# VectorE's exponential as two bf16 tiles that TensorE sums, in a pre-LN attention and GeGLU block

## The chip, the cores and the metric

The kernel runs on one core of one Trainium2 chip. The core has a matrix engine (TensorE, PE in the profile; PEld is its weight load), a vector engine (VectorE, DVE), an engine for functions such as the exponential (ScalarE, ACT), a general engine (GpSimd, POOL) and SyncE (SP), which here only issues DMAs. The metric is device time in microseconds of one execution; the time before is the median of three runs.

## The reference

One transformer block over a sequence of S = 2048 rows of D = 640, with 32 heads of 20, and a gated feed-forward part of width 1728, all in bf16:

```python
x = A_x
h = x + _A_ref(_layernorm(x, axis=-1), A_wqkv, A_wo)
h2 = h + _B_ref(_layernorm(h, axis=-1), B_w_gate, B_w_up, B_w_down)
# _A_ref: qkv = x @ wqkv; scores = q k^T * 20 ** -0.5; p = softmax(scores)
#         o = p v; o @ wo
# _B_ref: g = x @ w_gate; u = x @ w_up; (gelu_tanh(g) * u) @ w_down
```

The exponentials are the bulk of the elementwise work: 32 x 2048 x 2048 of them, which are 2048 tiles of 128 keys by 512 queries.

## The kernel before

The kernel lists its operations with their dependencies, planned durations and priorities, and a planner inside it (`Sched.schedule`) walks through planned time and fixes the order of instructions on each engine and the PSUM bank of each result. On the chip every engine then runs its own list in order and waits on semaphores. Almost every instruction is issued from one place, so most groups of the profile carry the line of that helper (L429); the matmuls of QK are at L1072, the evacuations on VectorE of its share of the scores at L996, gate and up at L1275, down at L1393.

Attention goes by **slots** (33 of them). A slot is a range of queries and one or more groups of four heads: 512 queries and one group, 256 and two, or 128 and four; each holds 16 **quads**, and a quad is four tiles, one for each head of a group. The scores of a tile are one bank of PSUM. TensorE computes QK with the four heads in four row strips of its array (contraction 32) and PV in four column strips (21 output rows: 20 of the head and one of ones, which gives the softmax's sum). The bound that takes the place of the row maximum enters through one extra row of Q, with the constant `OFF`.

Most tiles go to ScalarE in **units** of three and two tiles alternately (banks 0 to 2 and 3 to 4; two and two in slots 28 and 29): one Exp of 1536 or 1024 columns each (`unit`). Some quads go to VectorE instead. `D_QUADS` says how many in each slot, `D_LEAD` how many tiles ahead of their slot they start, and `D_LAG` how many units after a quad's last QK its PV is put into the list. Such a tile uses bank 7 or 5, which it shares with the background matmuls. `d_exp` evacuates it as int16: the scaled score is an exponent and a mantissa's fraction in fixed point. Two tiles, or from slot 16 on four, are then corrected together in five or six more instructions: mask the fraction, a linear step, a square, a product, an addition to the integer, and a last scaling that makes the bits of a bf16 number. In the slots named in `DA_SLOTS` the addition is done by a DMA that GpSimd issues and that accumulates in SBUF (`accum_op=ALU.add`). PV then takes the one bf16 tile (`pv_op`).

The feed-forward part of a chunk of rows (six **chunks** of 256 and four of 128) is background work that fills TensorE's and VectorE's lists between the attention's slots (`post`, `down`). Its GELU has three forms. In plain form the gate matmuls are copied to SBUF and ScalarE runs GELU in long instructions, with a load of another function table ahead of and behind it; chunks in `MERGE` hold their gates until the next chunk's are there, so that both share the loads. Chunks in `TANH` use tanh, which shares a table with Exp, and some more instructions on VectorE. The last chunk (the tail) runs after the last exponential.

Where the planner finds TensorE too idle for its clock to stay up, it adds filler matmuls of zeros to the PV accumulation (`pad`, in the profile `ps<-kt_all,zer`) or to a free bank (`warm`).

Of the kernel before, what the change touches and what calls it, by code (L numbers as in the profile page):

```python
# [7 lines left out]
ALU = mybir.AluOpType  # L8
# [362 lines left out]
OFF = 63.0 * 0.6931471805599453 / SCALE  # L371

OCT = 512.0
EXP_MUL = SCALE * 1.4426950408889634 * OCT
CA, CB, CC = -0.277383, 1.25604202, 1.0 - 11.0 / 128
PV_QUADS = 2
D_LAG = 12
MERGE = (0, 2)
TANH = (4, 6, 7, 8)
# [7 lines left out]
DA_ISSUE, DA_LAT = 0.95, 7  # L387
DA_SLOTS = (1, 10, 11, 12, 14, 15, 16, 18, 19, 20, 22, 23, 27, 28, 31)
PR, PR2 = 12, 6
D_QUADS = (0, 2, 2, 2, 2, 2, 2, 2, 2, 2, 2, 2, 3, 2, 3, 2, 3, 2, 3, 2, 3, 2, 3, 2, 2, 2, 3, 2, 3, 2, 2, 2, 0)  # L390
D_FIRST, D_PART = 2, 0.55
D_LEAD = ((0, 0, 0, 0, 0, 0, 0, 0), (0, 10, 20, 36, 36, 36, 36, 40, 36, 36, 32, 36, 36, 36, 36, 36, 40, 36, 32, 36, 40, 36, 36, 32, 36))
D_WIDE = 16
D_G = (7, 8)
# [13 lines left out]
def bass_sequential_preLN__mha_block__glu_gated_geglu__prompt_kernel(  # L408
# [12 lines left out]
    with ExitStack() as es:  # L421
# [93 lines left out]
        dv = [ka[:, 1024 * i:1024 * i + 1024].bitcast(I16) for i in range(2)]  # L515
        dvw = [ka.bitcast(I16)]
        pts2 = carve(PR2 * 512)


        carve = carver(qt_all[:, 0, :, :].rearrange("p g s -> p (g s)"), NG * 512)  # L520
        dv += [carve(1024).bitcast(I16) for _ in range(2)]
        df1 = carve(1024)
        dw1 = [carve(1024), dwx[:, 1024:2048]]
        carve = carver(qt_all[:, 0, :, :].rearrange("p g s -> p (g s)"), NG * 512)
        dvw += [carve(2048).bitcast(I16) for _ in range(2)]
        dv += [dvx[:, 1024 * i:1024 * i + 1024].bitcast(I16) for i in range(2)]
        dvw.append(dvx[:].bitcast(I16))
        zb = dvx[:, 0:1024].rearrange("p (i s) -> p i s", i=2)
        dv0 = [ha_f[:, 1024 * i:1024 * i + 1024].bitcast(I16) for i in range(5)]
        dv0.append(hnT.rearrange("p a s -> p (a s)")[:, 1024:2048].bitcast(I16))  # L530
        df0 = ha_f[:, 5120:6144]
        dw0 = [ha_f[:, 6144:7168], hnT.rearrange("p a s -> p (a s)")[:, 0:1024]]
        carve = carver(qt_all[:, 1, :, :].rearrange("p g s -> p (g s)"), NG * 512)
        df2 = carve(2048)
        dw2 = [carve(2048), dwx[:]]
        carve = carver(qt_all[:, 2, :, :].rearrange("p g s -> p (g s)"), NG * 512)
        dvw += [carve(2048).bitcast(I16) for _ in range(2)]
# [404 lines left out]
        d_cur, d_now = [None], [None]  # L942
        d_alt = [0]
        d_late = []
# [11 lines left out]
        def q_done(k):  # L956
            return sum((tuple(last_qk[c]) for c, (q0, _) in enumerate(QR) if q0 // 512 == k), ())

        def d_kind(tile, u):
            if tile[0] in (7, 8) and units[u][0][0] in D_G:  # L960
                return "g"
            return "e" if tile[0] < e_end else "f" if tile[0] < 8 else "l" if tile[0] < D_WIDE else "w"

        def d_free(tile):
            kind = d_now[0]
            return sum((tuple(sc.rd.get((x, t), ())) for x in ("aq", "sel") for t in range(NA)), ()) if kind == "g" else \
                tuple(sc.rd.get(("aq", 2), ())) + tuple(sc.rd.get(("aq", 3), ())) if kind == "l" else \
                tuple(t_last.get(4, ())) if kind == "w" and d_cur[0][1] > 3 else ()

        def d_pick(tile, u):  # L970
            if len(d_raw) == 0:
                d_now[0] = kind = d_kind(tile, u)
                busy = set(x[1][1] for x in d_done)
                busy |= set(("w", k) for k, ks in enumerate(((0, 1), (2, 3), (), (4, 5))) if any(("l", x) in busy for x in ks))
                n_ = {"e": 6, "f": 3, "g": 4, "l": 6, "w": 6 if QR[slots[units[u][0][0]][0]][0] >= 1536 else 4}[kind]
                pool = {"f": [("e", 4), ("l", 0), ("l", 1)], "g": [("l", i) for i in (0, 1, 4, 5)]}.get(kind) or [(kind, i) for i in range(n_)]
                pool = [p for p in pool if p not in busy]
                assert pool
                d_cur[0] = min(pool, key=lambda p: d_last.get(p, -1))
                d_last[d_cur[0]] = len(d_ops)  # L980
            i, kind = d_cur[0], d_now[0]
            return tuple(e_ops) + (q_done(0) if kind in "lw" else ()) + (q_done(1) + tuple(d_late) + tuple(t_last.get(2, ())) if kind == "w" else ()) + \
                (q_done(2) if kind == "w" and i[1] > 3 else ()) + \
                d_free(tile)

        def d_exp(b, tile, prio, u, aft):

            kind = d_now[0]
            n = 4 if kind == "w" else 2
            h = len(d_raw)  # L990
            i = d_cur[0]
            v = {"e": dv0, "l": dv, "w": dvw}[i[0]][i[1]]
            df, dw = {"e": (df0, dw0), "f": (df0, dw0[:1]), "g": (dwx[:, 0:1024], dw1[1:]), "l": (df1, dw1), "w": (df2, dw2)}[kind]
            keys = [("dv", i)] + ([("dv", ("l", k)) for k in ((0, 1), (2, 3), (), (4, 5))[i[1]]] if kind == "w" and i[1] < 4 else [])
            held = sum((tuple(sc.rd.get(k, ())) + ((sc.lw[k],) if k in sc.lw else ()) for k in keys), ())
            d_ops.append(op("dve", lambda eng: eng.tensor_scalar(v[:, 512 * h:512 * h + 512], bank(b), EXP_MUL, -32000.0,  # L996
                                                                 ALU.mult, ALU.max), c_dve(512), P_QK,
                            reads=[("SD", tile)], writes=[("dvq", i, h)], rel=[b], after=aft + held))
            d_raw.append(tile)
            if kind != "w":  # L1000
                d_late[:] = d_ops[-8:]
            if h < n - 1:
                return
            zi = df.bitcast(I16)
            d_alt[0] += 1
            a_ = d_alt[0] % len(dw)
            dk = ("dw", 1 if kind == "g" else a_)
            dw = dw[a_]
            di, dw = dw.bitcast(I16), dw.bitcast(F16)
            w_ = len(d_raw) / 2  # L1010
            d = lambda fn, n, r, w: d_ops.append(op("dve", fn, 0.066 + n * w_, prio, reads=r, writes=w))
            d(I("tensor_scalar", zi, v, 511, 2048, ALU.bitwise_and, ALU.bitwise_or), 0.265, [("dvq", i, k) for k in range(n)], ["df"])
            d(I("tensor_scalar", dw, zi, CA / OCT, CB, ALU.mult, ALU.add), 0.265, ["df"], [dk])
            d(I("tensor_tensor", dw, dw, dw, ALU.mult), 0.53, [dk], [dk])
            if tile[0] in DA_SLOTS:
                d(I("tensor_tensor", di, dw, zi, ALU.mult), 0.53, ["df", dk], [dk])
                d_ops.append(op(POOL, I("dma_start", v, di, accum_op=ALU.add), DA_ISSUE, prio, reads=[dk], writes=[("dv", i)],
                                sem="da%s%d" % i, lat=DA_LAT * (w_ + 1) / 3))
            else:
                d(I("tensor_tensor", dw, dw, zi, ALU.mult), 0.53, ["df", dk], [dk])  # L1020
                d(I("tensor_tensor", v, v, dw, ALU.add), 0.53, [dk, ("dv", i)], [("dv", i)])
            d(I("tensor_scalar", v, v, 0.25, 16256.0 + 128.0 * (CC - 1.0), ALU.mult, ALU.add), 0.265, [("dv", i)], [("dv", i)])
            if kind != "w":
                d_late[:] = d_ops[-8:]
            for k, tl in enumerate(d_raw):
                d_done.append((v[:, 512 * k:512 * k + 512].bitcast(BF16), ("dv", i), tl))
            d_raw.clear()
# [20 lines left out]
        def unit(u):  # L1048
# [47 lines left out]
            if six:  # L1096
                bd = bks[2]
            elif xd:
                bd = Bank(*BG[tl[0][0]])
                nd = 512 // QR[slots[xd[0]][0]][1]  # L1100
                qd = op("pe", [qk_mms(lambda: bank(bd), xd, kk) for kk in range(nd)], SD_ALONE,
                        P_SD, mode="row", util=0.0533, reads=qk_reads(xd), writes=[("SD", xd)], acq=[bd], after=d_free(xd) + ((prev,) if prev is not None else ()))
                sc.small[qd] = (xd[3], nd, qk)
                last_qk[slots[xd[0]][0]].append(qd)
            n = 512 * na
            pk = [("P", p0 + i) for i in range(na)]
            exp_ops.append(op("act", I("activation", pt, PS[:, 512 * s0:512 * s0 + n], ACT.Exp, scale=SCALE),
               c_act(n), P_QK, mode="exp", reads=[("S", u)], writes=pk, rel=bks[0:na], after=e_ops if p0 >= PR else ()))
            if xd:
                d_exp(bd, xd, P_EPI, u, aft)  # L1110
# [387 lines left out]
```

## Time and profile before

| | |
|---|---|
| runs | 896.44, 899.02, 898.96 us; median 898.96 |
| profiled execution | span 895.2 us; no time of its own beside the span is given |
| ACT busy | 864.5 us (97%) |
| PE busy | 850.3 us (95%) |
| DVE busy | 781.8 us (87%) |
| POOL busy | 113.8 us (13%) |
| granted clock of TensorE | 9 of 9 tenths in all 40 slices |
| DMA issued by GpSimd | 19.40 MB, 12.1% of the 16 engines |
| ACT table loads | 10, 1.28 us each |

How to read it: a group's row gives line, engine, operation, output and input tiles and shapes, and the count; then busy time and the mean length of one in ns; then the idle time of the engine ahead of them and what ended most of it. ACT's and DVE's instructions overlap a little with the next one, so the sum of their lengths is above their busy time, and the pace is read from starts. A matmul's end is modelled, so TensorE's busy time is not its load.

### The profile page before, as it was taken

The page shows a single profiled execution, that of the slowest core. Times are in us where ns is not written, and L with a number is a line of the kernel's source. Part 1 is how long each engine was busy: PE and PEld are TensorE (multiplying, and loading weights), DVE is VectorE, ACT ScalarE, POOL GpSimd, SP SyncE. Part 2 cuts the span into 40 slices and gives each one's busy share as a digit, 9 for nine tenths or more (in the row PEclk, how much of TensorE's full clock was granted, in tenths as well). Part 3 has the DMA queues.
Part 4 walks back from the last instruction along what each step waited for, and adds up shares of the span by engine and source line. Part 5 has one row for each costly group of instructions (what it writes and reads, how often), then busy time and mean ns, then how long its engine had stood idle before and what let it go on. Part 6 is the DMA issues. An engine that isn't in the chain of part 4 may idle for free.

```text
span 895.2 us, 28750 instructions
## 1 busy us (share of the span) xinstructions
PE 850.3 (95%) x12892; PEld 426.0 (48%) x12892; DVE 781.8 (87%) x1456; ACT 864.5 (97%) x809; POOL 113.8 (13%) x245
## 2 busy tenths in 40 slices
PE   4999999999899999999998999999999999999998
PEld 2432332234344454444333454444555666667677
DVE  7748999998899988999699978998998899899863
ACT  7999999999999999999999999999999999999992
POOL 6601000000210111202112000021001021010200
PEclk9999999999999999999999999999999999999999
DMA  7214111453420223223240222414120103320110
GB/s 264 77 30 87 31 50 32 136 153 82 125 74 16 38 48 78 44 40 70 49 87 16 49 48 56 86 16 89 41 37 18 33 11 63 60 55 11 41 27 23
DMA packets 46106, 53.55 MB, mean 60 GB/s; under 512 B 19076, under 2 KB 37616, under 8 KB 45984
## 3 DMA queue, kind: packets, MB, share of 16 engines
q1 hardware_dynamic: 38640, 32.32, 13.4%
q0 software_dynamic: 7344, 19.40, 12.1%
q8 instruction: 101, 1.65, 0.8%
q14 instruction: 21, 0.17, 0.1%
HBM read 20.12 MB, written 8.09 MB: 32 GB/s over the span
## 4 chain that ended last, share of the span: by engine, by line
ACT 52%; PE 28%; DVE 15%; POOL 3%; issue 1%; DMA 1%; SPq 0%; POOLq 0%; ACTq 0%
ACT pts L429 33%; ACT rege L429 18%; PE ps L1072 8%; PE ps L735 6%; PE ps L429 5%; PE ps L1275 4%; DVE rege L429 3%; PE ps L1393 2%; DVE qt_all L429 2%; DVE rege L996 2%; DVE dwx L429 1%; POOL nw L429 1%; DVE dvx L996 1%; DVE qt_all L996 1%; DVE stats L429 1%
## 5 line engine op out<-in xcount | busy, mean ns | idle before, releaser
L429 ACT ACTIVATE pts<-ps 128x1536 bf16<-128x1536 f32 (+1 forms) x480 | 561.2, 1320 | 3.9 <-PE ps L1072 2.0
L1072 PE MATMUL ps<-qt_all,kt_all 32*128 32x256 bf16 (+2 forms) x4736 | 319.4, 257 | 17.9 <-ACT pts L429 7.6
L429 ACT ACTIVATE rege<-ps 128x1536 bf16<-128x1536 f32 (+1 forms) x238 | 289.6, 1322 | 1.5 <-PE ps L1072 1.4
L1072 PEld LDWEIGHTS ps<-qt_all,kt_all 32*128 32x128 bf16 x4736 | 121.5, 92 | 212.2 <-ACT pts L429 96.7
L1275 PE MATMUL ps<-rege,regw 128*128 128x256 bf16 (+1 forms) x1400 | 163.4, 253 | 5.0 <-DVE rege L1362 1.7
L1275 PEld LDWEIGHTS ps<-rege,regw 128*128 128x128 bf16 x1400 | 103.1, 98 | 51.6 <-issue 24.2
L429 PE MATMUL ps<-pts,v_all 128*21 128x256 bf16 (+2 forms) x2722 | 123.1, 260 | 0.0
L996 DVE TENSOR_SCALAR qt_all<-ps 128x512 int16<-128x512 f32 x112 | 76.2, 685 | 20.3 <-PE ps L1072 19.8
L429 PE MATMUL ps<-rege,v_all 128*21 128x256 bf16 (+2 forms) x1550 | 90.3, 263 | 0.1
L735 PE MATMUL ps<-regw 128*128 128x512 bf16 (+1 forms) x350 | 86.0, 352 | 1.2 <-DVE rs L429 1.0
L1393 PE MATMUL ps<-regw,rege 128*128 128x320 bf16 x448 | 82.1, 302 | 0.1
L996 DVE TENSOR_SCALAR rege<-ps 128x512 int16<-128x512 f32 x108 | 73.2, 685 | 9.6 <-PE ps L1072 8.9
L429 DVE TENSOR_TENSOR qt_all<-qt_all 128x2048 f16<-128x2048 f16 (+5 forms) x77 | 75.5, 981 | 0.9
L429 PEld LDWEIGHTS ps<-pts,v_all 128*21 128x21 bf16 x2722 | 58.5, 91 | 29.7 <-issue 23.9
L429 DVE TENSOR_SCALAR qt_all<-qt_all 128x2048 int16<-128x2048 int16 (+5 forms) x122 | 64.2, 532 | 4.8 <-DMA qt_all<-qt_all 3.0
L429 PE MATMUL ps<-kt_all,zer 128*32 128x512 bf16 x684 | 58.6, 385 | 1.3 <-DVE osb L429 1.3
L1393 PEld LDWEIGHTS ps<-regw,rege 128*128 128x128 bf16 x448 | 36.8, 98 | 28.8 <-issue 11.7
L429 PEld LDWEIGHTS ps<-rege,v_all 128*21 128x21 bf16 x1550 | 39.6, 91 | 18.6 <-issue 12.7
L735 PEld LDWEIGHTS ps<-regw 128*128 128x128 bf16 x350 | 27.4, 98 | 42.0 <-issue 25.7
L429 DVE TENSOR_TENSOR rege<-rege 128x1024 f16<-128x1024 f16 (+1 forms) x68 | 46.3, 680 | 0.4
L429 DVE TENSOR_TENSOR dwx<-dwx 128x1024 f16<-128x1024 f16 (+1 forms) x51 | 45.1, 884 | 0.9
L996 DVE TENSOR_SCALAR dvx<-ps 128x512 int16<-128x512 f32 x60 | 40.3, 684 | 3.8 <-PE ps L1072 3.3
(136 smaller groups left out, 808.2 us busy)
## 6 DMA issues: line engine op xcount, KB each, us to landing
qt_all<-dwx POOLq DMA_DIRECT2D x7, 512.0 KB, 4.7
qt_all<-qt_all POOLq DMA_DIRECT2D x6, 512.0 KB, 4.7
dvx<-qt_all POOLq DMA_DIRECT2D x6, 512.0 KB, 5.0
q_rows<-regw SPq DMA_DIRECT2D x20, 128.0 KB, 1.8
out_dram<-rege SPq DMA_DIRECT2D x16, 160.0 KB, 2.2
regw<-in_A_wqkv_dram SPq DMA_DIRECT2D x3, 800.0 KB, 11.6
rege<-in_A_x_dram SPq DMA_DIRECT2D x7, 320.0 KB, 3.5
regw<-in_B_w_gate_dram SPq DMA_DIRECT2D x5, 432.0 KB, 3.7
```

The lines of the kernel that those rows point to most:

```text
L429: return lambda eng: getattr(eng, method)(*args, **kwargs)
L735: yield op("pe", lambda eng, l=l, r=r, k=k: eng.matmul(bank(bk, n), l, r, start=(k == 0), stop=(k == len(steps) - 1)), c_mm(n) + cold, pri ...
L996: d_ops.append(op("dve", lambda eng: eng.tensor_scalar(v[:, 512 * h:512 * h + 512], bank(b), EXP_MUL, -32000.0, ALU.mult, ALU.max), c_dve( ...
L1072: return lambda eng: eng.matmul(out()[:, kk * nq:(kk + 1) * nq], kt_all[32 * j:32 * j + 32, g, kt * 128:(kt + 1) * 128], qt_all[32 * j:32 ...
L1275: op("pe", lambda eng, a=a, f=f, fi=fi: eng.matmul(bank(bk)[:, fi * nq:(fi + 1) * nq], w[:, a, F0[f]:F0[f] + 128], hnT[:, a, 128 * tb:128 ...
L1393: op("pe", lambda eng, f=f, o=o, hf=hf, bk=bk: eng.matmul(bank(bk, 320), ha_f[:, o:o + 128], wd[:, f, hf * 320:(hf + 1) * 320], start=(f = ...
```

## The change

The exponential on VectorE gets another form. `EXP_MUL` and `OFF` are set so that the int16 of a tile, v, is at once the bit pattern of a bf16 number, 2^e (1 + m). Three instructions over four tiles follow: y = the fraction of v with the exponent of one half, 0.5 (1 + m); y = v x y, which is 2^(e-1) (1 + m)^2; and v = the exponent of v with a constant last bit, 2^e (1 + 1/128). The sum y + v is close to a constant times 2^(e+m); the constant is matched on ScalarE by the bias of its Exp (`E_BIAS`). The sum is never formed: PV runs once over y and once over v, both into the same accumulation. The accumulating DMAs are gone, as is the shorter two-tile form.

With it come: 78 quads on VectorE where there were 70, `D_LAG` 2 for 12, other leads, one pool of spare SBUF regions (a quad takes two of 2048 columns) for the hand-made sets, `TANH` of two chunks (7, 8) for four (4, 6, 7, 8), and `MERGE` of (0, 2, 5) for (0, 2), so that chunk 4 runs a plain GELU alone and chunks 5 and 6 share one.

```diff
-OFF = 63.0 * 0.6931471805599453 / SCALE
-OCT = 512.0
-EXP_MUL = SCALE * 1.4426950408889634 * OCT
+OFF = (127.0 + 63.0) * 0.6931471805599453 / SCALE
+EXP_MUL = SCALE * 1.4426950408889634 * 128.0
+E_BIAS = 0.41005255 - 127.0 * 0.6931471805599453
-D_LAG = 12
-MERGE = (0, 2)
-TANH = (4, 6, 7, 8)
+MERGE = (0, 2, 5)
+TANH = (7, 8)
-D_QUADS = (0, 2, 2, 2, 2, 2, 2, 2, 2, 2, 2, 2, 3, 2, 3, 2, 3, 2, 3, 2, 3, 2, 3, 2, 2, 2, 3, 2, 3, 2, 2, 2, 0)
-D_FIRST, D_PART = 2, 0.55
-D_LEAD = ((0, 0, 0, 0, 0, 0, 0, 0), (0, 10, 20, 36, 36, 36, 36, 40, 36, 36, 32, 36, 36, 36, 36, 36, 40, 36, 32, 36, 40, 36, 36, 32, 36))
+D_LAG = 2
+D_QUADS = (0, 2, 3, 2, 2, 3, 2, 2, 3, 3, 3, 3, 3, 3, 2, 3, 2, 3, 4, 3, 2, 3, 3, 3, 2, 2, 2, 2, 2, 2, 2, 2, 0)
+D_FIRST, D_PART = 2, 0.8
+D_LEAD = ((0, 0, 0, 0, 0, 0, 0, 0), (0, 10, 12, 12, 12, 12, 12, 12, 12, 12, 12, 16, 16, 8, 8, 8, 12, 12, 12, 12, 12, 12, 12, 12, 8))
...
+            d_ops.append(op("dve", lambda eng: eng.tensor_scalar(v[:, 512 * h:512 * h + 512], bank(b), EXP_MUL, 0.0, ALU.mult, ALU.max),
+                            c_dve(512), P_QK, reads=[("SD", tile)], writes=[vk[h]], rel=[b], after=aft))
...
-            d(I("tensor_scalar", zi, v, 511, 2048, ALU.bitwise_and, ALU.bitwise_or), 0.265, [("dvq", i, k) for k in range(n)], ["df"])
-            d(I("tensor_scalar", dw, zi, CA / OCT, CB, ALU.mult, ALU.add), 0.265, ["df"], [dk])
-            d(I("tensor_tensor", dw, dw, dw, ALU.mult), 0.53, [dk], [dk])
-            if tile[0] in DA_SLOTS:
-                d(I("tensor_tensor", di, dw, zi, ALU.mult), 0.53, ["df", dk], [dk])
-                d_ops.append(op(POOL, I("dma_start", v, di, accum_op=ALU.add), DA_ISSUE, prio, reads=[dk], writes=[("dv", i)],
-                                sem="da%s%d" % i, lat=DA_LAT * (w_ + 1) / 3))
-            else:
-                d(I("tensor_tensor", dw, dw, zi, ALU.mult), 0.53, ["df", dk], [dk])
-                d(I("tensor_tensor", v, v, dw, ALU.add), 0.53, [dk, ("dv", i)], [("dv", i)])
-            d(I("tensor_scalar", v, v, 0.25, 16256.0 + 128.0 * (CC - 1.0), ALU.mult, ALU.add), 0.265, [("dv", i)], [("dv", i)])
+            d(I("tensor_scalar", y, v, 0x7F, 0x3F00, ALU.bitwise_and, ALU.bitwise_or), 0.53, vk, yk)
+            d(I("tensor_tensor", y.bitcast(BF16), v.bitcast(BF16), y.bitcast(BF16), ALU.mult), 1.06, vk + yk, yk)
+            d(I("tensor_scalar", v, v, 0x7F80, 1, ALU.bitwise_and, ALU.bitwise_or), 0.53, vk, vk)
...
-            exp_ops.append(op("act", I("activation", pt, PS[:, 512 * s0:512 * s0 + n], ACT.Exp, scale=SCALE),
+            exp_ops.append(op("act", I("activation", pt, PS[:, 512 * s0:512 * s0 + n], ACT.Exp, bias=E_BIAS, scale=SCALE),
...
-                            d_pv.setdefault(s_, []).append(pv_op(s_, [have], [], [], pv_first[s_], ("OD", q)))
+                            for m in range(2):
+                                d_pv.setdefault(s_, []).append(pv_op(s_, [[(x[0][m], x[1][m], x[2]) for x in have]], [], [], pv_first[s_], ("OD", q)))
```

More of the change, by code (lines that the diff above doesn't have):

```diff
@@ L369 @@
 LN_EPS = 1e-5
-OFF = 63.0 * 0.6931471805599453 / SCALE
-OCT = 512.0
-EXP_MUL = SCALE * 1.4426950408889634 * OCT
-CA, CB, CC = -0.277383, 1.25604202, 1.0 - 11.0 / 128
+OFF = (127.0 + 63.0) * 0.6931471805599453 / SCALE
+EXP_MUL = SCALE * 1.4426950408889634 * 128.0
+E_BIAS = 0.41005255 - 127.0 * 0.6931471805599453
 PV_QUADS = 2
-D_LAG = 12
-MERGE = (0, 2)
-TANH = (4, 6, 7, 8)
+MERGE = (0, 2, 5)
+TANH = (7, 8)
 W_EARLY = 4
@@ L386 @@
 P_TANH = -1
-DA_ISSUE, DA_LAT = 0.95, 7
-DA_SLOTS = (1, 10, 11, 12, 14, 15, 16, 18, 19, 20, 22, 23, 27, 28, 31)
 PR, PR2 = 12, 6
-D_QUADS = (0, 2, 2, 2, 2, 2, 2, 2, 2, 2, 2, 2, 3, 2, 3, 2, 3, 2, 3, 2, 3, 2, 3, 2, 2, 2, 3, 2, 3, 2, 2, 2, 0)
-D_FIRST, D_PART = 2, 0.55
-D_LEAD = ((0, 0, 0, 0, 0, 0, 0, 0), (0, 10, 20, 36, 36, 36, 36, 40, 36, 36, 32, 36, 36, 36, 36, 36, 40, 36, 32, 36, 40, 36, 36, 32, 36))
-D_WIDE = 16
-D_G = (7, 8)
+D_PRIO = 2
+D_Q2 = 26
+D_LAG = 2
+D_QUADS = (0, 2, 3, 2, 2, 3, 2, 2, 3, 3, 3, 3, 3, 3, 2, 3, 2, 3, 4, 3, 2, 3, 3, 3, 2, 2, 2, 2, 2, 2, 2, 2, 0)
+D_FIRST, D_PART = 2, 0.8
+D_LEAD = ((0, 0, 0, 0, 0, 0, 0, 0), (0, 10, 12, 12, 12, 12, 12, 12, 12, 12, 12, 16, 16, 8, 8, 8, 12, 12, 12, 12, 12, 12, 12, 12, 8))
 T_DVE = (0, 1, 3, 5, 9, 10, 11, 12, 13, 14)
@@ L514, in bass_sequential_preLN__mha_block__glu_gated_geglu__prompt_kernel @@
         ka = carve(2048)
-        dv = [ka[:, 1024 * i:1024 * i + 1024].bitcast(I16) for i in range(2)]
-        dvw = [ka.bitcast(I16)]
         pts2 = carve(PR2 * 512)
[L520 to L527, printed above, removed]
-        zb = dvx[:, 0:1024].rearrange("p (i s) -> p i s", i=2)
[L529 to L537, printed above, removed]
+        zb = dvx[:, 0:1024].rearrange("p (i s) -> p i s", i=2)
+        qr = [qt_all[:, k, :, :].rearrange("p g s -> p (g s)") for k in range(3)]
+        hn = hnT.rearrange("p a s -> p (a s)")
+        spare = {"h": [ha_f[:, 0:2048], ha_f[:, 2048:4096], hn[:, 0:2048]], "i": [ha_f[:, 4096:6144]], "k": [ka], "x": [dvx[:]], "w": [dwx[:]],
+                 **{"q%d" % k: [qr[k][:, 0:2048], qr[k][:, 2048:4096]] for k in range(3)}}
         kdr = nc.dram_tensor("k_rows", [D, S], BF16, kind="Internal").ap()
@@ L941, in bass_sequential_preLN__mha_block__glu_gated_geglu__prompt_kernel @@
         d_last = {}
-        d_cur, d_now = [None], [None]
-        d_alt = [0]
-        d_late = []
+        d_cur = []
         t_last = {}
@@ L957, in q_done, with d_regions @@
             return sum((tuple(last_qk[c]) for c, (q0, _) in enumerate(QR) if q0 // 512 == k), ())
[L959 to L968, printed above, removed]
+        def d_regions(tile, u):
+            us = units[u][0][0]
+            if tile[0] < e_end:
+                return ("h", "i")
+            assert us >= 7
+            return ("i",) * (tile[0] == 7) + ("k", "x", "w") + ("q0",) * (us >= 8) + ("q1",) * (us >= 16) + ("q2",) * (us >= D_Q2)
@@ L970, in d_pick, with d_free @@
+        def d_free(region):
+            if region in ("h", "i", "k"):
+                return tuple(e_ops)
+            if region in ("x", "w"):
+                return tuple(e_ops) + sum((tuple(sc.rd.get((x, t), ())) for x in ("aq", "sel") for t in range(NA)), ())
+            return q_done(int(region[1])) + tuple(t_last.get(4, ()) if region == "q2" else ())
         def d_pick(tile, u):
             if len(d_raw) == 0:
-                d_now[0] = kind = d_kind(tile, u)
-                busy = set(x[1][1] for x in d_done)
@@ L974, in d_pick @@
[L974 to L984, printed above, removed]
+                busy = set(y[0] for x in d_done for y in x[1])
+                free = [p for p in ((r, i) for r in d_regions(tile, u) for i in range(len(spare[r]))) if p not in busy]
@@ L986, in d_exp @@
+                assert len(free) > 1, (tile, u, busy)
+                d_cur[:] = sorted(free, key=lambda p: d_last.get(p, -1))[:2]
+                for p in d_cur:
+                    d_last[p] = len(d_ops)
+            return sum((d_free(p[0]) for p in d_cur), ())
         def d_exp(b, tile, prio, u, aft):
-            kind = d_now[0]
-            n = 4 if kind == "w" else 2
             h = len(d_raw)
-            i = d_cur[0]
-            v = {"e": dv0, "l": dv, "w": dvw}[i[0]][i[1]]
-            df, dw = {"e": (df0, dw0), "f": (df0, dw0[:1]), "g": (dwx[:, 0:1024], dw1[1:]), "l": (df1, dw1), "w": (df2, dw2)}[kind]
@@ L994, in d_exp @@
[L994 to L998, printed above, removed]
+            v, y = [spare[r][i].bitcast(I16) for r, i in d_cur]
@@ L999, in d_exp @@
+            vk, yk = [[(p, k) for k in range(4)] for p in d_cur]
+            d_ops.append(op("dve", lambda eng: eng.tensor_scalar(v[:, 512 * h:512 * h + 512], bank(b), EXP_MUL, 0.0, ALU.mult, ALU.max),
+                            c_dve(512), P_QK, reads=[("SD", tile)], writes=[vk[h]], rel=[b], after=aft))
             d_raw.append(tile)
-            if kind != "w":
-                d_late[:] = d_ops[-8:]
-            if h < n - 1:
+            if h < 3:
                 return
-            zi = df.bitcast(I16)
@@ L1005, in d_exp @@
[L1005 to L1011, printed above, removed]
-            d(I("tensor_scalar", zi, v, 511, 2048, ALU.bitwise_and, ALU.bitwise_or), 0.265, [("dvq", i, k) for k in range(n)], ["df"])
-            d(I("tensor_scalar", dw, zi, CA / OCT, CB, ALU.mult, ALU.add), 0.265, ["df"], [dk])
@@ L1022, in d_exp @@
-            d(I("tensor_scalar", v, v, 0.25, 16256.0 + 128.0 * (CC - 1.0), ALU.mult, ALU.add), 0.265, [("dv", i)], [("dv", i)])
-            if kind != "w":
-                d_late[:] = d_ops[-8:]
+            d = lambda fn, k, r, w: d_ops.append(op("dve", fn, 0.066 + k, prio, reads=r, writes=w, after=aft))
+            d(I("tensor_scalar", y, v, 0x7F, 0x3F00, ALU.bitwise_and, ALU.bitwise_or), 0.53, vk, yk)
+            d(I("tensor_tensor", y.bitcast(BF16), v.bitcast(BF16), y.bitcast(BF16), ALU.mult), 1.06, vk + yk, yk)
@@ L1025, in d_exp @@
+            d(I("tensor_scalar", v, v, 0x7F80, 1, ALU.bitwise_and, ALU.bitwise_or), 0.53, vk, vk)
             for k, tl in enumerate(d_raw):
-                d_done.append((v[:, 512 * k:512 * k + 512].bitcast(BF16), ("dv", i), tl))
+                d_done.append(([x[:, 512 * k:512 * k + 512].bitcast(BF16) for x in (y, v)], (yk[k], vk[k]), tl))
             d_raw.clear()
@@ L1101, in unit @@
                 qd = op("pe", [qk_mms(lambda: bank(bd), xd, kk) for kk in range(nd)], SD_ALONE,
-                        P_SD, mode="row", util=0.0533, reads=qk_reads(xd), writes=[("SD", xd)], acq=[bd], after=d_free(xd) + ((prev,) if prev is not None else ()))
+                        P_SD, mode="row", util=0.0533, reads=qk_reads(xd), writes=[("SD", xd)], acq=[bd], after=aft + ((prev,) if prev is not None else ()))
                 sc.small[qd] = (xd[3], nd, qk)
@@ L1106, in unit @@
             pk = [("P", p0 + i) for i in range(na)]
-            exp_ops.append(op("act", I("activation", pt, PS[:, 512 * s0:512 * s0 + n], ACT.Exp, scale=SCALE),
+            exp_ops.append(op("act", I("activation", pt, PS[:, 512 * s0:512 * s0 + n], ACT.Exp, bias=E_BIAS, scale=SCALE),
                c_act(n), P_QK, mode="exp", reads=[("S", u)], writes=pk, rel=bks[0:na], after=e_ops if p0 >= PR else ()))
             if xd:
-                d_exp(bd, xd, P_EPI, u, aft)
+                d_exp(bd, xd, D_PRIO, u, aft)
             pv_wait.extend((pt[:, 512 * i:512 * i + 512], ("P", p0 + i), tl[i]) for i in range(na))
```

## The prediction

> **What bounds the kernel now.** I read the page first, then the waits of ScalarE (ACT), then its groups by shape and the chain of work in order of time, and last the stages. From the page:
>
> ```profile
> span 895.2 us, 28750 instructions
> PE 850.3 (95%) x12892; PEld 426.0 (48%) x12892; DVE 781.8 (87%) x1456; ACT 864.5 (97%) x809; POOL 113.8 (13%) x245
> ACT  7999999999999999999999999999999999999992
> ACT 52%; PE 28%; DVE 15%; POOL 3%; issue 1%; DMA 1%; SPq 0%; POOLq 0%; ACTq 0%
> ```
>
> ACT is full in every slice but the first and the last, and half of the chain that ended last is its own work. Three engines are above 85%, so the next question is whether ACT waits for the others. Its waits, the rows that fall between its first exponential (31.2 us) and its last (872 us):
>
> ```profile
> ACT pts L429 <- PE ps L1072: 2.0, 4, 0.9
> ACT pts L429 <- PE ps L429: 1.8, 2, 1.5
> ACT rege L429 <- PE ps L1072: 1.4, 2, 1.0
> ```
>
> In 841 us ACT waits about 5.2 us. So ACT is the bound there, and the outside parts (31 us ahead of the first exponential, 23 us behind the last) are latency that this change hardly touches. What counts is what the change does to ACT's work, and whether PE and DVE can still feed it.
>
> **ACT, exponentials.** Its groups by shape, and its pace in the chain, start and length of merged runs of instructions:
>
> ```profile
> L429 ACT ACTIVATE pts<-ps 128x1536 bf16<-128x1536 f32 x222 | 344.2, 1551 | 3.1 <-PE ps L429 1.8 <-PE ps L1072 1.2
> L429 ACT ACTIVATE pts<-ps 128x1024 bf16<-128x1024 f32 x258 | 284.8, 1122 | 0.8 <-PE ps L1072 0.8
> L429 ACT ACTIVATE rege<-ps 128x1536 bf16<-128x1536 f32 x110 | 170.8, 1553 | 1.5 <-PE ps L1072 1.4
> L429 ACT ACTIVATE rege<-ps 128x1024 bf16<-128x1024 f32 x128 | 141.9, 1123 | 0.0
> ```
>
> ```profile
> 430.57 4.52 ACT pts L429 x4
> ...
> 773.71 5.50 ACT pts L429 x6
> ```
>
> 332 units of three tiles and 386 of two are 1768 tiles of 512 columns; with the 280 that DVE takes (70 quads of four) that is all 2048. The means (1.55, 1.12 us) hold an overlap with the neighbour. The chain has the pace: six 1024s in 5.50 us, 0.917 each; two pairs of 1536 and 1024 in 4.52 us, so 1.343 for a 1536. The change gives DVE 78 quads. Running through the loop that fills the units with the new D_QUADS and D_LEAD, by count alone, leaves 325 units of three, 380 of two and one of one. That is 7 x 1.343 + 6 x 0.917 less, and one 512 more (0.917 - 0.426 = 0.49): **-14.4 us**.
>
> **ACT, table loads.** Chunks 4 and 6 leave the tanh form, and chunk 5 is merged with 6, so the GELU groups between exponentials go from three (0+1, 2+3, 5) to four (0+1, 2+3, 4, 5+6). Timeline of one such group:
>
> ```profile
> 309.55 1.05 ACT L429 ACTIVATE pts<-ps 128x1024 bf16<-128x1024 f32 x1
> ...
> 310.62 1.28 ACT L429 ACT_TABLE_LOAD   x1
> ...
> 311.91 6.46 ACT L429 ACTIVATE rege<-rege 128x2048 bf16<-128x2048 bf16 x4
> ...
> 318.38 1.28 ACT L429 ACT_TABLE_LOAD   x1
> ...
> 319.68 2.37 ACT L429 ACTIVATE rege<-ps 128x1536 bf16<-128x1536 f32 x2
> ```
>
> From the end of one function to the start of the next is 1.31 us (310.60 to 311.91, 318.37 to 319.68), and the 0.1 to 0.2 us by which neighbours overlap is lost once or twice. Two loads more: **+2.8 us**. The Trainium skill's page "ScalarE: Activation LUTs", section "What ACT_TABLE_LOAD costs", gives about 1283 ns for the load and some 1380 ns of drain, 2.66 us for every switch; the trace agrees with the load and shows no drain of that size behind a running stream. By the page two switches would be 5.3 us and the time 889; I take the trace.
>
> **ACT, GELU against tanh.** Chunk 4 had seven 512-wide tanh, chunk 6 three and a 256:
>
> ```profile
> 863.27 1.15 ACT L429 ACTIVATE qt_all<-qt_all 128x512 f16<-128x512 f16 x2
> ...
> 864.09 1.24 ACT L429 ACTIVATE pts<-ps 128x1024 bf16<-128x1024 f32 x1
> ```
>
> Here one 512 and one 256 hold ACT from 863.27 to 864.09, 0.82 us; with 0.426 per 512 columns that is 0.52 and 0.30. Ten and one go: -5.5 us. Their GELUs come back in long form: 3.23 us for chunk 4 (half of the 6.46 above), about 1.6 for the 1792 columns of chunk 6: +4.8. Net **-0.7 us**.
>
> ACT in sum: -14.4 + 2.8 - 0.7 = **-12.3 us**.
>
> **ACT, the bias.** Exp gets bias=E_BIAS, a plain number where the default was zero. If it were fetched from memory it would cost something; two ACT groups of 512 columns, without a fetched bias and with one (one0), show how much:
>
> ```profile
> L778 ACT ACTIVATE regw<-ps 128x512 bf16<-128x512 f32 x5 | 3.0, 595 | 0.8 <-PE ps L735 0.7
> L799 ACT ACTIVATE kt_all<-ps,one 128x512 bf16<-128x512 f32 x2 | 1.4, 688 | 0.8 <-PE ps L794 0.8
> ```
>
> 0.093 us each. A number in the instruction I cost at nothing; the other case is a rival below.
>
> **DVE.** Means of its instructions, and two that stand back to back:
>
> ```profile
> L996 DVE TENSOR_SCALAR qt_all<-ps 128x512 int16<-128x512 f32 x112 | 76.2, 685 | 20.3 <-PE ps L1072 19.8
> L429 DVE TENSOR_TENSOR qt_all<-qt_all 128x2048 f16<-128x2048 f16 x26 | 31.6, 1214 | 0.2
> L429 DVE TENSOR_SCALAR qt_all<-qt_all 128x2048 int16<-128x2048 int16 x44 | 29.9, 680 | 0.3
> L429 DVE TENSOR_TENSOR rege<-rege 128x1024 f16<-128x1024 f16 x44 | 30.0, 681 | 0.3
> L429 DVE TENSOR_SCALAR rege<-rege 128x1024 int16<-128x1024 int16 x62 | 24.8, 418 | 0.2
> ```
>
> ```profile
> 309.10 0.69 DVE L996 TENSOR_SCALAR rege<-ps 128x512 int16<-128x512 f32 x1
> ...
> 309.71 0.68 DVE L1348 CAST rege<-ps 128x512 bf16<-128x512 f32 x1
> ```
>
> 0.61 from start to start where each is shown with 0.69, so 0.08 is overlap: 0.61, 1.13, 0.60, 0.60, 0.34. A quad before: four evacuations, 2.44, and either wide 3 x 0.60 + 2 or 3 x 1.13 (6.5 or 7.6) or in two halves (6.9 or 8.1), the smaller where a DMA does the last addition. By slots that is 14 x 6.9 + 18 x 8.1 + 23 x 6.5 + 15 x 7.6 = 506 us. After: 2.44 + 0.60 + 1.13 + 0.60 = 4.8, times 78 = 372. With the tanh chunks' extra DVE work (10.5 blocks at about 1.2) DVE loses some 145 of 782 us and stands near 73%. It is beside ACT, so this is worth nothing by itself; it can shorten waits for DVE, of which ACT's 5.2 us are the most that could come back. One POOL queue falls free of the accumulating DMAs; the LN steps on POOL behind them come sooner, with the same zero value. No SP transfer is moved.
>
> **PE.** Each DVE quad is now two PV quads. 32 PV matmuls of 128 columns (two quads), and the filler matmuls that keep the clock up:
>
> ```profile
> 872.48 0.63 PE L429 MATMUL ps<-pts,v_all 128*21 128x128 bf16 x32
> ```
>
> ```profile
> L429 PE MATMUL ps<-kt_all,zer 128*32 128x512 bf16 x684 | 58.6, 385 | 1.3 <-DVE osb L429 1.3
> ```
>
> 0.63 less the 0.22 of the last one's own length is 0.41 for two: 0.21 a quad where it follows other PV work, and, where it stands alone between other modes, the 0.39 that a filler set of four occupies at most. 78 of them: 16 to 30 us, I take 17, since both halves of a quad come free within one DVE instruction. What hides it, by stage: all work first, then the filler alone.
>
> ```profile
> 300.00:400.00 100.00, 97.47 (x1323) 48.55 (x1312) 92.24 (x186) 99.94 (x87) 16.41 (x29) 1.00 0.28 53
> ...
> 800.00:872.00 72.00, 71.12 (x1767) 51.79 (x1766) 61.45 (x123) 72.00 (x74) 5.39 (x16) 1.00 0.12 26
> ```
>
> ```profile
> 300.00:400.00 100.00, 4.43 (x52) 1.19 (x52) 0.00 (x0) 0.00 (x0) 1.00 0.28 53
> ...
> 800.00:872.00 72.00, 2.61 (x28) 0.63 (x28) 0.00 (x0) 0.00 (x0) 1.00 0.12 26
> ```
>
> The first two numbers behind the stretch's length are PE's and the count. These are the tightest stages: 4.4 of filler and 2.5 of idle time in 300 to 400, against about ten quads (2.1 to 3.9) and 1.5 of shrinkage; 2.6 and 0.9 in the last one, against some five quads. It fits, narrowly, so I cost it at **nothing**; without the cover it would be 17 us, and the gain gone. Merging chunk 5 with 6 holds back chunk 5's up and down matmuls (about 15 us of PE) by a slot or two; what of it is not done by 872 us would lengthen the end.
>
> **The sum.** 895.2 - 12.3 = 882.9 us of span. The times show three runs of 896.44 to 899.02; the median, 898.96, is 3.8 us above this span, so 886.7, said as **887 us**.
>
> **The rivals.**
> 1. The other side: the lag. PV of a DVE quad is put into PE's order two units after its last QK, where it was twelve. The chain behind the last evacuation is 0.60 + 1.13 + 0.60 = 2.3 us, two units are 2.26. Where DVE is late, PE stands at that PV with the next QK queued behind it, and ACT behind that. For it, PE already waited in this way:
>
> ```profile
> PE ps L429 <- DVE dvx L429: 2.3, 2, 1.3
> ```
>
> Against it, only twice, and DVE gets less loaded. At 12.3/78 = 0.16 us of ACT's time a quad the gain is gone; at 0.3 us it is 23 us, 910. Chance 0.11 that it ends slower.
> 2. PE runs short in some stages, ACT waits about a third of 17 us: 893. For it PE's 95%; against it the filler. 0.14.
> 3. The relief of DVE and POOL also removes most of ACT's 5.2 us and stalls at the GELU groups: 880. 0.14.
> 4. The change doesn't do what it says: the bias is fetched, 706 x 0.093 = 66 us: 953. The pages' rule speaks for the cheap case: "ScalarE: Activation LUTs", the same section of the Trainium skill, has 93 ns for each pointer operand and none for an immediate; the L778 and L799 rows agree on the 93. 0.02.
>
> **How the numbers follow.** The forecast has 0.59: 882 to 892, that is -12.3 with the loads and waits a few us either way. A measurement here tells about 0.3% (2.7 us) from no change. Faster: 0.59 + 0.14 + most of rival 2, 0.82. Same: the rest of rival 2, and rival 1 near its point of balance, 0.06. Slower: 0.12. The range reaches from rival 3's better half to the end of rival 2: 878 to 898.
>
> **What would show it.** Right: 325 + 380 + 1 exponentials on ACT, 12 table loads, pairs still at 2.26 us, ACT's waits for PE under 10 us, an isolated exponential no longer than before; DVE near 640 us; fewer than 684 filler matmuls; no accumulating DMA. Wrong: PE waiting at PV for DVE for many us with QK next (rival 1); filler near zero and ACT waiting for QK (rival 2); chunk 8's down matmuls well behind the last exponential.

## The result and the profile after

The changed kernel takes 882.41 us (881.89 to 882.65) beside 898.63 for the kernel before in the same session: a ratio of 0.9822, 95% interval 0.9808 to 0.9835. Measured again beside other experiments it gave 882.40 and 0.9828 (0.9814 to 0.9842). It is faster by 1.7 to 1.8%; 887 was forecast, with a range of 878 to 898. In the later sessions the executions of the kernel before fall into two groups, 896.2 to 897.3 us at a mean granted clock of 0.998 or more and 898.0 to 899.3 us at 0.996; the changed kernel's are all at 0.998 or more, and against the first group the gain is some 14.5 us.

The page of the changed kernel: span, busy times, the slices of DVE and ACT, and the engines' shares of the chain that ended last.

```profile
span 880.9 us, 29309 instructions
PE 844.7 (96%) x13370; PEld 430.9 (49%) x13370; DVE 645.9 (73%) x1117; ACT 852.1 (97%) x791; POOL 62.7 (7%) x194
DVE  7748877776898876877778976787776574666874
ACT  7999999999999999999999999999999999999991
ACT 67%; PE 27%; DVE 3%; POOL 2%; issue 1%; POOLq 0%
```

DVE fell from 782 to 646 us and ACT is as full as before, with a larger part of the chain. These are the groups of ACT by shape (count, busy time, mean ns, idle time ahead and its releaser) and, below them, a row of the chain in order of time:

```profile
L426 ACT ACTIVATE pts<-ps 128x1536 bf16<-128x1536 f32 x217 | 331.2, 1526 | 2.1 <-PE ps L426 1.5 <-PE ps L1023 0.2
L426 ACT ACTIVATE pts<-ps 128x1024 bf16<-128x1024 f32 x254 | 274.6, 1097 | 0.6 <-PE ps L1023 0.6
L426 ACT ACTIVATE rege<-ps 128x1536 bf16<-128x1536 f32 x108 | 164.6, 1524 | 0.2 <-PE ps L1023 0.2
L426 ACT ACTIVATE rege<-ps 128x1024 bf16<-128x1024 f32 x126 | 136.5, 1094 | 0.8 <-PE ps L1023 0.8
L426 ACT ACT_TABLE_LOAD x12 | 15.4, 1283 | 1.0 <-PEq L1435 0.8
```

```profile
58.90 4.52 ACT pts L426 x4
```

There are 325 units of three and 380 of two (and the single one), at the old pace of 4.52 us for two pairs, so the bias cost nothing. There are twelve table loads. The waits of ACT between its first and last exponential come to 3.3 us, where they were 5.2:

```profile
ACT pts L426 <- PE ps L426: 1.5, 1, 1.5
ACT rege L426 <- PE ps L1023: 1.0, 2, 0.8
...
ACT pts L426 <- PE ps L1023: 0.8, 3, 0.3
```

Where the 14.3 us between the two spans lie can be read from the last exponential's end, that is the start of the table load behind it: the timeline of ACT, before and then after.

```profile
869.64 2.47 ACT L429 ACTIVATE pts<-ps 128x1536 bf16<-128x1536 f32 x2
872.13 1.28 ACT L429 ACT_TABLE_LOAD   x1
```

```profile
855.13 1.94 ACT L426 ACTIVATE pts<-ps 128x1536 bf16<-128x1536 f32 x2
857.09 1.28 ACT L426 ACT_TABLE_LOAD   x1
```

The first exponential starts at 31.2 and 30.0 us, so the stretch of exponentials went from 840.9 to 827.1 us, 13.8 shorter; 1.2 were won ahead of it, and the end behind it grew by 0.7 (23.1 to 23.8). Starts of ACT's instructions summed by kind over that stretch give the same: the exponentials 807.5 to 791.9 (their waits included), table loads 12.95 to 15.53 (the whole run), GELU and tanh 25.6 to 24.9; together -13.8.

TensorE's filler went from 684 matmuls and 58.6 us to

```profile
L426 PE MATMUL ps<-kt_all,zer 128*32 128x512 bf16 x512 | 45.1, 385 | 0.2 <-DVE osb L426 0.2
```

### The profile page after: what moved, and what is told of

Same layout as the page of the kernel before. It is cut to its first block, busy times and chain, and to the rows that moved or that the text cites. A ratio compares the mean times of both kernels' runs of the same rounds, so it can differ in the third digit from the quotient of the medians.

```text
span 880.9 us, 29309 instructions
## 1 busy us (share of the span) xinstructions
PE 844.7 (96%) x13370; PEld 430.9 (49%) x13370; DVE 645.9 (73%) x1117; ACT 852.1 (97%) x791; POOL 62.7 (7%) x194
## 4 chain that ended last, share of the span: by engine, by line
ACT 67%; PE 27%; DVE 3%; POOL 2%; issue 1%; POOLq 0%
ACT pts L426 43%; ACT rege L426 23%; PE ps L1023 7%; PE ps L426 5%; PE ps L1227 5%; PE ps L716 4%; PE ps L1345 3%; ACT L426 1%; PE ps L658 1%; PE ps L1128 1%; DVE qt_all L967 1%; PE ps L821 1%; DVE qt_all L426 0%; POOL nw L426 0%; DVE stats L426 0%
## 5 line engine op out<-in xcount | busy, mean ns | idle before, releaser
L426 ACT ACTIVATE pts<-ps 128x1536 bf16<-128x1536 f32 (+1 forms) x472 | 547.1, 1293 | 2.7 <-PE ps L426 1.5
L426 ACT ACTIVATE rege<-ps 128x1536 bf16<-128x1536 f32 (+1 forms) x234 | 281.3, 1292 | 1.1 <-PE ps L1023 1.0
L967 DVE TENSOR_SCALAR qt_all<-ps 128x512 int16<-128x512 f32 x204 | 139.2, 687 | 62.7 <-PE ps L1023 61.9
L426 PE MATMUL ps<-rege,v_all 128*21 128x256 bf16 (+2 forms) x1698 | 99.6, 267 | 0.3 <-DVE rege L426 0.3
L426 PEld LDWEIGHTS ps<-rege,v_all 128*21 128x21 bf16 x1698 | 42.1, 91 | 23.8 <-issue 14.9
L967 DVE TENSOR_SCALAR rege<-ps 128x512 int16<-128x512 f32 x64 | 43.3, 686 | 12.8 <-PE ps L1023 12.3
L1314 DVE TENSOR_TENSOR rege<-rege,ps 128x512 bf16<-128x512 bf16 (+1 forms) x46 | 31.3, 679 | 25.1 <-PE ps L1227 25.1
L426 PE MATMUL ps<-kt_all,zer 128*32 128x512 bf16 x512 | 45.1, 385 | 0.2 <-DVE osb L426 0.2
L426 DVE TENSOR_SCALAR qt_all<-qt_all 128x2048 int16<-128x2048 int16 (+2 forms) x65 | 40.6, 629 | 0.3
L1300 DVE CAST rege<-ps 128x512 bf16<-128x512 f32 (+1 forms) x46 | 31.2, 679 | 9.2 <-PE ps L1227 9.2
L426 DVE COPY osb<-ps 128x512 f32<-128x512 f32 (+2 forms) x33 | 22.2, 672 | 18.2 <-PE ps L426 18.1
```

The source lines that it names most:

```text
L426: return lambda eng: getattr(eng, method)(*args, **kwargs)
L1300: cp.append(op("dve", lambda eng, bg=bg, fv=fv, w=w: eng.tensor_copy(fv, bank(bg, w)), c_dve(w), p, reads=[kg], writes=hkeys(k), rel=[bg], ...
L1314: hdone.append(op("dve", lambda eng, bu=bu, fv=fv, w=w: eng.tensor_tensor(fv, fv, bank(bu, w), ALU.mult), c_dve(w), p, reads=[ku] + hkeys( ...
```

## The experiments

Theory A was that of the prediction: ScalarE's work sets the time, and VectorE's and GpSimd's relief and TensorE's second PV lie beside it. The rivals were that the relief itself is the gain (B), that TensorE's extra work costs time (C), and others named in place. A hole is a wait of ACT between two exponentials. Each ratio is to the kernel before on the same chip in the same session, whose median there was 896.9 to 897.2 us.

**Fewer quads.** This is the changed kernel with the old counts.

```diff
-D_QUADS = (0, 2, 3, 2, 2, 3, 2, 2, 3, 3, 3, 3, 3, 3, 2, 3, 2, 3, 4, 3, 2, 3, 3, 3, 2, 2, 2, 2, 2, 2, 2, 2, 0)
+D_QUADS = (0, 2, 2, 2, 2, 2, 2, 2, 2, 2, 2, 2, 3, 2, 3, 2, 3, 2, 3, 2, 3, 2, 3, 2, 2, 2, 3, 2, 3, 2, 2, 2, 0)
```

> The changed kernel with the old 70 quads on VectorE; everything else of the change stays. The units are then again 332 of three tiles and 386 of two, 799.8 us of exponentials at the measured pace against 785.4. Theory A (the gain is ScalarE's work alone): 14.4 us above the changed kernel's 882.4, so 897 us, a ratio to before of about 0.998. Rival B (the gain is the relief of VectorE, GpSimd and the DMA queues, whatever the count): 882 to 886, ratio 0.98 to 0.985.

It took 903.75 us, ratio 1.0074 (1.0058 to 1.0091): slower than the kernel before, and 7 us more than theory A says. The timeline of its ACT shows what is extra:

```profile
814.06 1.94 ACT L426 ACTIVATE pts<-ps 128x1024 bf16<-128x1024 f32 x2
823.51 2.37 ACT L426 ACTIVATE pts<-ps 128x1024 bf16<-128x1024 f32 x2 [7.51 <-PE ps L1023]
```

There is one hole of 7.5 us, in which TensorE runs down and gate matmuls and the next QK stands behind them in its list. Less that hole the run would be at 896, an estimate. Why the planner put it there was not settled. So the eight quads were taken away elsewhere:

```diff
-D_QUADS = (0, 2, 3, 2, 2, 3, 2, 2, 3, 3, 3, 3, 3, 3, 2, 3, 2, 3, 4, 3, 2, 3, 3, 3, 2, 2, 2, 2, 2, 2, 2, 2, 0)
+D_QUADS = (0, 2, 2, 2, 2, 2, 2, 2, 2, 3, 2, 3, 3, 2, 2, 2, 2, 3, 4, 2, 2, 3, 2, 3, 2, 2, 2, 2, 2, 2, 2, 2, 0)
```

> The changed kernel with 70 quads again, but with the eight taken from slots 2, 5, 8, 10, 13, 15, 19 and 22, so that the late slots stay as in the changed kernel; the other 70-quad run had one hole of 7.5 us in ScalarE's list late in the run, that is in the order and not in the amount of work. Theory A (ScalarE's work): 882.4 + 14.4 = 897 us, less hole than 7.5 us, ratio about 0.998. Rival D (fewer quads cost more than their exponentials, 2.7 us each as in the first 70-quad run): 903 us or more.

It took 898.35 us, ratio 1.0007 (0.9997 to 1.0016), with a hole of 2.7 us at about the same time. At equal count the change as a whole gains nothing: rival B falls, and rival D (903 or more) too. The two spreads of 70 quads differ by 5.4 us (903.75 and 898.35), so the planner's order alone is worth some us.

**GELU as before.** Here only TANH and MERGE go back.

```diff
-MERGE = (0, 2, 5)
-TANH = (7, 8)
+MERGE = (0, 2)
+TANH = (4, 6, 7, 8)
```

> The changed kernel with the old TANH (4, 6, 7, 8) and MERGE (0, 2). Theory A: two table loads fewer (-2.8 us), tanh for GELU (+0.7): 880.3 us, ratio 0.9796. Rival: the tanh chunks' some 12 us of VectorE work and their waits come into the way of ScalarE, and 882.4 or more results; only then was this part of the change a gain.

It took 879.32 us, ratio 0.9798 (0.9784 to 0.9813). To tell it from the changed kernel, both were measured again side by side:

> The changed kernel once more, unchanged, beside the next one on the same chip: 882 us, ratio 0.982.

> The changed kernel with the old TANH and MERGE once more, beside the changed one: by theory A 2.1 us below it (two table loads saved, less tanh for GELU), by the first look 3 us; if the two come out alike, the table loads were hidden.

The changed kernel took 882.40 us, ratio 0.9828 (0.9814 to 0.9842), against 879.75, ratio 0.9799 (0.9783 to 0.9814): 2.65 us by the medians, where the sum said 2.1. The two intervals just touch, but no run of the one (881.91 to 882.76) reaches one of the other (878.48 to 880.80); the earlier pair, 882.41 and 879.32, has the same sign and size. So the rival falls, this part of the change costs time, and the changed kernel with the old GELU choice is the fastest of those run here.

**The form alone.** This kernel has 70 quads, spread as above, and the old GELU choice: of the change only the new form is left, with its leads, its regions and the other places of the 70 quads.

> The changed kernel with 70 quads spread as in the spread 70-quad run and with the old TANH and MERGE: only the new form of the exponential (and its leads) is left of the change. Theory A: ScalarE's work is that of the kernel before, so the time is that of before, 897 us within 2, though VectorE does some 130 us less and GpSimd's DMAs are gone. Rival B (the relief itself is worth something): 890 or less.

It took 894.25 us, ratio 0.9959 (0.9946 to 0.9972), which is 2.65 us faster: a little more than theory A allowed, and short of rival B's 890. Its waits of ACT within the exponentials are these, against the kernel before's 5.2 us:

```profile
ACT pts L426 <- PE ps L426: 1.5, 1, 1.5
...
ACT pts L426 <- PE ps L1023: 1.0, 2, 0.7
...
ACT rege L426 <- PE ps L1023: 0.5, 2, 0.3
```

They come to 3.0 us, so 2.2 us of waits went, most of the difference. How much of the 2.65 us is VectorE's relief (625 us busy where it was 782) and how much the other order was not separated; two orders of 70 quads differed by more. With that said, the change splits into form and order -2.65 (896.90 to 894.25), eight quads -14.5 (894.25 to 879.75), GELU +2.65 (879.75 to 882.40).

**VectorE at the old price.** The first of the three instructions is given five times over.

```diff
             d(I("tensor_scalar", y, v, 0x7F, 0x3F00, ALU.bitwise_and, ALU.bitwise_or), 0.53, vk, yk)
+            d(I("tensor_scalar", y, v, 0x7F, 0x3F00, ALU.bitwise_and, ALU.bitwise_or), 0.53, vk, yk)
+            d(I("tensor_scalar", y, v, 0x7F, 0x3F00, ALU.bitwise_and, ALU.bitwise_or), 0.53, vk, yk)
+            d(I("tensor_scalar", y, v, 0x7F, 0x3F00, ALU.bitwise_and, ALU.bitwise_or), 0.53, vk, yk)
+            d(I("tensor_scalar", y, v, 0x7F, 0x3F00, ALU.bitwise_and, ALU.bitwise_or), 0.53, vk, yk)
```

> The changed kernel in which the first of the three instructions of a VectorE quad (y = masked v) is given five times over, the same result each time: 4 x 0.60 = 2.4 us more a quad, which brings it from 4.8 to the 7.2 us of the old form; ScalarE's work and TensorE's matmuls stay. Theory A with VectorE as the limit: 187 us more on VectorE, 833 of 881 us; ScalarE begins to wait for it and the time is 900 to 950. Rival B' (VectorE is beside the path at any load under 100%): 882 to 886.

It took 966.0 us, ratio 1.0763 (1.0737 to 1.0788), beyond even the upper end of the 900 to 950 expected. These are its busy times, the engines' shares of its chain, and the longest waits of ACT:

```profile
PE 888.4 (92%) x13710; PEld 442.9 (46%) x13759; DVE 824.0 (86%) x1429; ACT 854.6 (89%) x791; POOL 74.2 (8%) x194
...
DVE 34%; ACT 30%; PE 29%; POOL 4%; issue 2%; DMA 1%; SPq 0%; POOLq 0%; ACTq 0%
```

```profile
ACT pts L426 <- PE ps L426: 47.2, 9, 14.1
ACT rege L426 <- PE ps L426: 19.7, 5, 9.8
```

ACT does the same work but waits in holes of up to 14 us for TensorE's PV. Two of these holes as stages (busy times of PE, PEld, DVE, ACT and POOL in turn):

```profile
115.90:123.30 7.40, 6.87 (x51) 2.21 (x52) 7.40 (x12) 0.05 (x2) 0.00 (x0) 1.00 0.16 53
285.90:300.00 14.10, 11.19 (x129) 7.28 (x130) 13.75 (x26) 0.04 (x2) 4.54 (x14) 1.00 0.12 24
```

DVE is busy for 7.40 of 7.40 and 13.75 of 14.10 us there, and its part of the chain is 34%, where it is 3% in the changed kernel. So VectorE is the limit in these stretches, as theory A said, though its mean over the span is 86%, and rival B' falls. Whether the spare regions, of which a quad keeps two until its PV, add to the holes was not varied.

At this price 78 quads cost 84 us more than in the changed kernel, so the cheap form is what makes the 14.5 possible. The old form itself with 78 quads, for which 890 to 910 us was expected with the new leads, has no time: it kept its own long leads, with which at some point of the plan no region is free for a quad, and shorter leads were not tried with it.

**One PV a quad.** The second PV is left out, so that half of the exponential's sum is missing in the output.

```diff
-                            for m in range(2):
+                            for m in range(1):
```

> The changed kernel without PV over the second of the two tiles of a VectorE quad: 78 x 4 PV tiles are left out, so the output lacks that half of the exponential's sum. Theory A (the second PV takes the place of filler): 882 us within 1, with more filler than the 512 of the changed kernel. Rival C (TensorE's extra PV is on the path): up to 17 us less, 866 to 878.

It took 884.45 us, ratio 0.9857 (0.9842 to 0.9872): 2 us more than with the second PV, not less. C falls for this count. The filler did not grow, as expected, but shrank, to 460 matmuls, and in one stage the granted clock (the third number from the end) dropped. This kernel's rows come first, the stage and the part of it at half clock, and then the changed kernel's:

```profile
200.00:300.00 100.00, 95.02 (x1306) 39.76 (x1303) 78.87 (x135) 97.19 (x86) 9.62 (x29) 0.97 0.25 65
272.90:279.70 6.80, 6.80 (x66) 1.83 (x63) 3.61 (x6) 4.70 (x4) 0.00 (x0) 0.50 0.01 2
```

```profile
200.00:300.00 100.00, 97.15 (x1470) 43.80 (x1469) 80.84 (x140) 99.52 (x89) 9.24 (x29) 1.00 0.27 74
```

For 6.8 us TensorE ran at half clock, and ACT (the fourth busy time) lost 2.3 us in the stage, which is the 2 us that the run is longer. That it was the missing PV that let the clock drop, so that in the changed kernel the second PV also does the filler's work, is likely but not shown: the planner's order changed with it, and the changed kernel's own first profile has 3.4 us at half clock too, near 740 us, its second none.

**The bias fetched.**

```diff
+        cst(I("memset", ebias[:], E_BIAS), "ebias", 1)
...
-            exp_ops.append(op("act", I("activation", pt, PS[:, 512 * s0:512 * s0 + n], ACT.Exp, bias=E_BIAS, scale=SCALE),
+            exp_ops.append(op("act", I("activation", pt, PS[:, 512 * s0:512 * s0 + n], ACT.Exp, bias=ebias[:, 0:1], scale=SCALE),
```

> The changed kernel with the bias of Exp fetched from a 128 x 1 tile in SBUF and not a number in the instruction. By the difference of the rows of 512 columns with and without a fetched bias (0.093 us) for 706 exponentials: 66 us more, 948 us. Rival: back to back the fetch is hidden behind the instruction in front, and 882 to 886 results.

It took 940.9 us, ratio 1.0482 (1.046 to 1.0505), 58.5 us above the changed kernel. This is a row of its chain of work:

```profile
82.90 4.87 ACT pts L426 x4
```

Four take 4.87 us for 4.52, which is 0.0875 us for each exponential, so hardly any of the 0.093 is hidden back to back, and the rival falls. 706 of them would be 62 us. The Trainium skill's page "ScalarE: Activation LUTs", section "What ACT_TABLE_LOAD costs", has about 93 ns for a pointer operand. In a running stream the trace shows a little less, 87.5 ns, and it shows the number in the instruction free (4.52 us before and after), as the page has it.

**More quads.** There is one more in slots 14, 16, 20, 24, 25 and 27.

```diff
-D_QUADS = (0, 2, 3, 2, 2, 3, 2, 2, 3, 3, 3, 3, 3, 3, 2, 3, 2, 3, 4, 3, 2, 3, 3, 3, 2, 2, 2, 2, 2, 2, 2, 2, 0)
+D_QUADS = (0, 2, 3, 2, 2, 3, 2, 2, 3, 3, 3, 3, 3, 3, 3, 3, 3, 3, 4, 3, 3, 3, 3, 3, 3, 3, 2, 3, 2, 2, 2, 2, 0)
```

> The changed kernel with 84 quads: one more in slots 14, 16, 20, 24, 25 and 27; 320 units of three and 376 of two, 10.9 us of exponentials less. Theory A alone: 871.5 us, ratio 0.970. Rival C (TensorE's room is used up late in the run, where filler is down to 2 to 3 us in 100): the late slots' PV and the background matmuls come too late, ScalarE waits, and the time is 882 or more.

It took 890.25 us, ratio 0.9923 (0.9905 to 0.9941), 8 us above the changed kernel. Rival C is right here, but not by waits of the exponentials. Around the last of them the timeline reads:

```profile
843.37 1.08 ACT L426 ACTIVATE rege<-ps 128x1024 bf16<-128x1024 f32 x1
...
844.46 1.28 ACT L426 ACT_TABLE_LOAD   x1
...
847.52 6.27 PE L1227 MATMUL ps<-rege,regw 128*128 128x128 bf16 x107
```

The exponentials end at 844.4, 12.6 us ahead of the changed kernel: 11.2 of it are the exponentials themselves, where theory A says 10.9, and 1.2 are tanh that moved behind them. But 43.7 us follow, where 23.8 did. In those stages TensorE is busy for 93 and 88% (the first number behind the length); this kernel's row, then the changed one's:

```profile
844.50:888.20 43.70, 40.64 (x564) 35.00 (x561) 25.78 (x66) 11.98 (x17) 0.00 (x0) 1.00 0.07 20
```

```profile
857.10:880.90 23.80, 20.83 (x267) 16.92 (x265) 9.58 (x24) 5.43 (x9) 0.00 (x0) 1.00 0.06 22
```

There are twice the matmuls, 564 for 267. Of gate and up there are 400, where the changed kernel has the last chunk's 140, and of down 112 for 76: most of the gate and up work of the two chunks before the last found no place under the exponentials and follows behind them.

## Why the prediction was right

- **ACT, exponentials, -14.4 us.** Right: -14.5 between two kernels that differ in the eight quads alone. The runs of one kernel scatter by 1.3 and 2.3 us there, so an agreement to 0.1 us is partly luck.
- **Table loads +2.8, GELU against tanh -0.7.** Right in kind and nearly in size: +2.1 forecast, +2.65 measured. In the stretch of exponentials the two loads took 2.6 us more, 1.29 each from start to start, and GELU and tanh 0.8 less; the rest lies in ACT's waits and in the end, which was 23.1 us long with the old GELU choice and 23.9 in the changed kernel, measured side by side. The longer price of the Trainium skill (2.66 us a switch; "ScalarE: Activation LUTs", "What ACT_TABLE_LOAD costs") would have made it 4.6.
- **The bias, nothing.** Right. The rival's price of 66 us measured 58.5 where the bias was fetched.
- **DVE, nothing by itself, at most the 5.2 us of waits.** This is the term of the sum that was mis-sized: the form, with the order that came with it, is worth 2.65 us, within the bound, and I took zero. So rival 3 came true in part: 1.9 of the 5.2 us of waits went in the changed kernel. Beside ACT's 13.8 us of the stretch there are the 1.2 ahead of the first exponential, a part that no edit aimed at: the first exponential starts at 29.8 to 31.2 us in the profiles, and at 30.0 and 30.7 in two of the changed kernel.
- **PE, nothing.** Right at 78: the filler fell by 13.5 us, and leaving the second PV out gained nothing. ACT's waits of 3.3 us leave no room for rival 2. DVE was put at 640 us and measured 646.
- **The lag.** Rival 1 did not come: PE's waits for DVE at the PV of DVE's quads are 0.7 and 0.3 us in all:

```profile
PE ps L426 <- DVE qt_all L426: 0.7, 2, 0.4
...
PE ps L426 <- DVE rege L426: 0.3, 1, 0.3
```

The forecast of 887 was 4.6 us too high, and 882.41 lies at the lower edge of its 882 to 892. 2.65 of it is the form's. Some 2.1 of it is the zero of the comparison: I put the median of 898.96 beside the span of another, faster execution and so added 3.8 us to the span, where span and time of one execution of the changed kernel differ by 1.7 (880.9 and 882.6). In the later sessions the kernel before stood at 896.9 to 897.2, from which the gain is 14.5. From there the sum's 12.3, with the form's 2.65 and without the 0.55 by which the GELU part cost more, gives 14.4.

What the prediction did not see is the other side of PE. I looked for TensorE running short as ACT waiting inside the stages. The 84-quad run shows that it comes out at the end instead, as background work left over.

## What to carry to other kernels

Where one engine is full, count its instructions at the pace of its chain before and after; here that gave the part of the eight quads well within a microsecond (14.4 and 14.5), while an engine at 87% that was relieved of 157 us at equal count, in another order, gave 2.65. The worth of a cheaper form on another engine is what work it lets you move there, so test it at equal count first. When a list of background work fills the gaps of a second engine, the price of more work on it may show not as waits but as the length of what follows the last instruction of the bound, as it did with 84 quads.

## What the runs showed of the hardware that was not expected

A fetched bias adds 0.0875 us to each exponential even back to back (4.87 for 4.52 us a four), 58.5 us in all. A run with fewer real matmuls on TensorE was longer: with one PV a quad there were 6.8 us at half clock, and ACT worked 2.3 us less in that stage than in the changed kernel. VectorE held up ScalarE at a mean of 86% busy: in two holes of 7.4 and 14.1 us it was busy for 7.40 and 13.75.
